# An elementwise layer-scale kernel: pieces of 40, 37, 40 and 11 rows, two large stores, and stores released by a load's landing

## Chip, cores, metric

One core of one Trainium2 chip. The metric is the device time of one execution in microseconds. "Span" is the time from the first to the last instruction in a profile; the time lies about 1.3 us above it. All runs told here are of the fast state, at a granted clock of 1.0. Ratios are the mean time of one kernel's fast runs over the mean of the other's of the same rounds, so they are not quite the ratios of the medians that stand beside them.

A packet is one record of a DMA engine's work in the trace: start, length, size, queue. The records as kept do not name the engine, so what is said of one engine is either a sum over all packets divided by 16 ("the mean engine", "an engine") or found by matching each packet's start to an earlier packet's end. A load or store is issued by its queue, runs as packets, and lands when its completion signal comes. A hole is time in which the DMA engines stand still.

## The reference

```python
B, S, D = 1024, 16, 512          # all bfloat16
def reference(x, y, gamma):      # x, y: [B, S, D]; gamma: [D]
    return x + gamma * y
```

33.55 MB must be read and 16.78 MB written, and there is one product and one sum per element.

## The kernel before

Each of 128 partitions holds 128 rows of 512 elements (1 KB a row). y stays whole in SBUF and becomes the result in place; x passes through a buffer of 64 rows. gamma is spread over the partitions by one matmul with a column of ones. The load queue (SP) and the store queue (ACT) are lists; VectorE makes a product and a sum per piece.

```python
PIECES = [32, 32, 32, 32]
X_AT = [0, 32, 0, 32]            # where a piece of x lies in its buffer
X_AFTER = [-1, -1, 0, 1]         # the sum that must be done before it may be overwritten
SP = [('x', 0), ('y', 0), ('x', 1), ('y', 1), ('y', 2), ('x', 2), ('y', 3), ('x', 3)]
# ('s', first piece, last piece, sum that releases it)
ACT = [('g',), ('s', 0, 0, 2), ('s', 1, 1, 2), ('s', 2, 2, 2), ('s', 3, 3, 3)]
# ... cut ...
            need = X_AFTER[args[0]] if kind == "x" else args[2] if kind == "s" else -1
            if need > known:
                eng.wait_ge(s_add, need + 1)
# ... cut ...
    for c in range(n):
        yt = y_sb[:, piece(c), :]
        _take(s_y[c], 16, nc.vector)
        nc.vector.tensor_tensor(
            out=yt, in0=yt, in1=gamma_sb[:, None, :].to_broadcast([P, PIECES[c], D]), op=MULT
        ).then_inc(s_dve, 1)
        _take(s_x[c], 16, nc.vector)
        _take(s_dve, 1, nc.vector)
        nc.vector.tensor_tensor(out=yt, in0=x_tile(c), in1=yt, op=ADD).then_inc(s_add, 1)
```

The first three stores are held back until the third sum (index 2) is done, although the first piece is ready much earlier, so that loads go first and stores after.

## Time and profile before

| | before |
|---|---|
| time, median of 3 runs | 120.31 us (120.3 to 120.99) |
| profiled execution: time, span | 120.87 us, 119.5 us |

The lines of the profile and their reading stand in the prediction below.

### The profile page before, as it was taken

The numbers are of one execution on the slowest core, as the hardware profiler recorded it, in microseconds if no ns is written. First come the engines' busy times: TensorE is split into PE (matmuls) and PEld (weight loads), VectorE is DVE, ScalarE is ACT, GpSimd is POOL, SyncE is SP. The second block draws the span as 40 slices with busy tenths as digits, with TensorE's granted clock in tenths as the row PEclk, the third lists the DMA queues.
The fourth block names the chain that finished last, engine by engine and source line by source line (L and its number), as shares of the span: only waits on it lengthen the run. The fifth ranks groups of instructions, "written<-read, shape, count | busy, mean of one in ns | idle before, by whom it ended". The sixth has DMA issues, their size and how long they took to land. (4 is left out here: it accounts for less than half of the span.)

```text
span 119.5 us, 84 instructions
## 1 busy us (share of the span) xinstructions
PE 0.6 (0%) x1; PEld 0.1 (0%) x1; DVE 70.2 (59%) x10; POOL 0.2 (0%) x4
## 2 busy tenths in 40 slices
PE   0100000000000000000000000000000000000000
PEld 0000000000000000000000000000000000000000
DVE  0100000699999289999999999999999600000000
POOL 0000000000000000000000000000000000000000
DMA  7989898998998989898989999898989898989995
GB/s 208 494 373 504 351 526 351 384 493 351 384 493 351 526 351 526 351 515 362 493 384 471 406 428 450 384 493 351 526 351 526 351 526 351 515 362 471 406 471 230
DMA packets 1730, 50.33 MB, mean 421 GB/s; under 512 B 193, under 2 KB 194, under 8 KB 194
## 3 DMA queue, kind: packets, MB, share of 16 engines
q1 hardware_dynamic: 1152, 33.55, 66.4%
q10 hardware_dynamic: 578, 16.78, 32.5%
HBM read 33.56 MB, written 16.78 MB: 421 GB/s over the span
## 5 line engine op out<-in xcount | busy, mean ns | idle before, releaser
L115 DVE TENSOR_TENSOR y_sb<-y_sb,gamma_sb 128x16384 bf16<-128x16384 bf16 x4 | 34.8, 8688 | 18.4 <-DVEq L22 18.4
L120 DVE TENSOR_TENSOR y_sb<-x_sb,y_sb 128x16384 bf16<-128x16384 bf16 x4 | 34.8, 8692 | 0.6
L109 DVE CAST gamma_sb<-gamma_ps 128x512 bf16<-128x512 f32 x1 | 0.7, 692 | 3.4 <-DVEq L22 3.4
L104 DVE MEMSET ones_row<- 1x128 bf16 x1 | 0.2, 165 | 2.0 <-PEq L38 2.0
L107 PE MATMUL gamma_ps<-gamma_row,ones_row 1*128 1x512 bf16 x1 | 0.6, 580 | 4.8 <-PEq L22 4.8
L107 PEld LDWEIGHTS gamma_ps<-gamma_row,ones_row 1*128 1x128 bf16 x1 | 0.1, 100 | 4.8 <-issue 4.8
L149 POOL MEMSET const-bfloat16-1.0<- 128x1 bf16 x1 | 0.1, 101 | 0.0
L149 POOL MEMSET const-uint8-127<- 128x1 uint8 x1 | 0.1, 101 | 0.0
L149 POOL MEMSET const-float32-0.0<- 128x1 f32 x1 | 0.1, 98 | 0.2 <-issue 0.2
L149 POOL MEMSET const-float32-1.0<- 128x1 f32 x1 | 0.1, 98 | 0.0
## 6 DMA issues: line engine op xcount, KB each, us to landing
x_sb<-in_x_dram SPq DMA_DIRECT2D x4, 4096.0 KB, 21.5
y_sb<-in_y_dram SPq DMA_DIRECT2D x4, 4096.0 KB, 35.4
out_dram<-y_sb ACTq DMA_DIRECT2D x4, 4096.0 KB, 23.8
gamma_row<-in_gamma_dram ACTq DMA_DIRECT2D x1, 1.0 KB
```

Of the source, the lines that this page charges most:

```text
L104: nc.vector.memset(ones_row, 1.0).then_inc(s_ones, 1)
L107: nc.tensor.matmul(gamma_ps, ones_row, gamma_row, start=True, stop=True).then_inc(s_ps, 1)
L109: nc.vector.tensor_copy(out=gamma_sb, in_=gamma_ps).then_inc(s_dve, 1)
L115: nc.vector.tensor_tensor(out=yt, in0=yt, in1=gamma_sb[:, None, :].to_broadcast([P, PIECES[c], D]), op=MULT).then_inc(s_dve, 1)
L120: nc.vector.tensor_tensor(out=yt, in0=x_tile(c), in1=yt, op=ADD).then_inc(s_add, 1)
L149: nc = _bacc.Bacc("TRN2", target_bir_lowering=False, num_devices=1)
```

## The change

The intent: let the stores start when the loads are nearly through, by a signal from the loads themselves and not by a sum that happens to end then, so that pieces may have any size; and use fewer, larger transfers (7 loads and 2 stores in place of 8 and 4). The buffer of x grows from 64 to 77 rows. "64 KB" is per partition.

```diff
-PIECES = [32, 32, 32, 32]
-SP = [('x', 0), ('y', 0), ('x', 1), ('y', 1), ('y', 2), ('x', 2), ('y', 3), ('x', 3)]
-ACT = [('g',), ('s', 0, 0, 2), ('s', 1, 1, 2), ('s', 2, 2, 2), ('s', 3, 3, 3)]
+PIECES = [40, 37, 40, 11]
+# ('x', first row, end row, place in the buffer), ('y' or 's', first row, end row)
+SP = [('x', 0, 40, 0), ('y', 0, 40), ('x', 40, 77, 40), ('y', 40, 77), ('y', 77, 128), ('x', 77, 117, 0), ('x', 117, 128, 40)]
+ACT = [('g',), ('s', 0, 64), ('s', 64, 128)]
+RELEASE = ('x', 77, 117, 0)
 # ... cut: bookkeeping of which rows a load or a store meets ...
+            if kind == "s" and not went:
+                _take(s_go, 1, eng)          # ACT, ahead of the first store
+                went = True
 # ... cut ...
+    _take(s_load[RELEASE], 16, nc.tensor)    # TensorE sees the landing ...
+    nc.tensor.sem_inc(s_go, 1)               # ... and tells ACT
+    nc.tensor.sem_inc(s_rel, 1)              # ... and VectorE
```

## The prediction

> **What bounds the kernel now.** I read the page first, parts 1 to 3, then the table of windows, then the order of time around the hand-over from loads to stores, and last the packet records of the trace (start, duration and size of each DMA packet).
>
> ```profile
> PE 0.6 (0%) x1; PEld 0.1 (0%) x1; DVE 70.2 (59%) x10; POOL 0.2 (0%) x4
> DMA  7989898998998989898989999898989898989995
> q1 hardware_dynamic: 1152, 33.55, 66.4%
> q10 hardware_dynamic: 578, 16.78, 32.5%
> L115 DVE TENSOR_TENSOR y_sb<-y_sb,gamma_sb 128x16384 bf16<-128x16384 bf16 x4 | 34.8, 8688 | 18.4 <-DVEq L22 18.4
> L120 DVE TENSOR_TENSOR y_sb<-x_sb,y_sb 128x16384 bf16<-128x16384 bf16 x4 | 34.8, 8692 | 0.6
> ```
>
> The two DMA queues took 66.4 + 32.5 = 98.9% of the span of all 16 engines: loads first (q1), stores second (q10). VectorE is busy 59%, and it sets nothing as long as it is in time. So the bound is the DMA engines, and the question is only which of their microseconds are not transfer at full rate. The windows answer that (columns: stretch, length, busy time of the engines, clock, DMA share, GB/s; 12.10 us is ten packets of 32 KB per engine):
>
> ```profile
> 0.00:1.00 1.00, 0.00 (x0) 0.00 (x0) 0.00 (x0) 0.20 (x4) 1.00 0.12 33
> 1.00:3.07 2.07, 0.00 (x0) 0.00 (x0) 0.17 (x1) 0.00 (x0) 1.00 1.14 348
> 3.07:15.20 12.13, 0.58 (x1) 0.10 (x1) 0.69 (x1) 0.00 (x0) 1.00 1.01 435
> 19.00:31.10 12.10, 0.00 (x0) 0.00 (x0) 8.89 (x2) 0.00 (x0) 1.00 0.97 395
> 43.20:55.30 12.10, 0.00 (x0) 0.00 (x0) 11.95 (x2) 0.00 (x0) 1.00 1.00 433
> 67.40:79.50 12.10, 0.00 (x0) 0.00 (x0) 11.95 (x3) 0.00 (x0) 1.00 1.00 433
> 79.50:91.60 12.10, 0.00 (x0) 0.00 (x0) 11.95 (x2) 0.00 (x0) 1.00 1.00 433
> 103.70:115.80 12.10, 0.00 (x0) 0.00 (x0) 0.00 (x0) 0.00 (x0) 1.00 1.00 433
> ```
>
> Loads alone, loads beside VectorE, and stores all run at 433 GB/s, and the window across the hand-over (79.50 to 91.60) does too: there is no hole between loads and stores. By the packet records, a 32 KB packet follows the last one on its engine every 1.210 us. The 96 packets of an engine at that pace are 116.2 us. The rest of 119.5 is four items: about 1.1 us before the first packets; 0.7 us by which each engine's first packet is long (1.93 against 1.21 us); about 1.1 us in a slow stage from 16 to 42 us, where packets take 1.22 to 1.33 us (the window with 395; its cause isn't shown, and VectorE's work isn't it, for later windows have more of that at 433); and about 0.5 us from the last packet's end to the end of the span. They add up to 119.6.
>
> The hand-over, in order of time (three merged issues, the third alone, then the last):
>
> ```profile
> 77.05 8.68 DVE L115 TENSOR_TENSOR y_sb<-y_sb,gamma_sb 128x16384 bf16<-128x16384 bf16 x1
> 77.17 4.06 ACTq L95 DMA_DIRECT2D out_dram<-y_sb  x3
> ...
> 78.04 3.19 ACTq L95 DMA_DIRECT2D out_dram<-y_sb  x1
> ...
> 85.88 8.69 DVE L120 TENSOR_TENSOR y_sb<-x_sb,y_sb 128x16384 bf16<-128x16384 bf16 x1
> 94.61 0.34 ACTq L95 DMA_DIRECT2D out_dram<-y_sb  x1
> ```
>
> The third addition ends at 77.13 and releases three stores at 77.17. The packet records have the first store packets at 80.1, just as the load queue runs dry (its last packet ends at 80.4). The last store is issued at 94.61, while the three before it keep the engines busy to about 109: 14 us of slack.
>
> **What the Trainium skill says.** "DMA: Bandwidth & Descriptors", section "Where 436 GB/s comes from", gives a ceiling of 435.2 GB/s for the 16 ports; the 433 here is 99.5% of it. The same page, "Why small descriptors are slow", names a fixed cost of about 3 cycles per packet. The difference between 1.210 us and 32768 B at 27.2 GB/s (1.2047 us) is 5.6 ns per packet, which is of that order. Its section "Queues, rings and completion order" says an engine switches between queues after each packet. This trace doesn't show such mixing: no store packet ran in the 2.9 us after the issue while load packets were left. "Advanced Engine Details and Errata", "VectorE Performance Modes", allows tensor_tensor two elements a cycle at best; 16384 elements in 8.69 us is 1.89 per ns, so the additions and products can't be made faster by other piece sizes.
>
> **The change, part by part.** The bytes are the same: 33.55 MB in, 16.78 MB out.
>
> 1. Fewer, larger packets. The loads go from 8 to 7 and the stores from 4 to 2, of 8 packets per engine each: 96 become 72. 24 x 5.6 ns = 0.13 us saved. It assumes that 64 KB per partition is one packet; if it is cut, less.
> 2. The work before the first packet, the long first packet and the tail are untouched: same two early loads, same kind of last store. 0.
> 3. The release of the stores. Now: landing of the load of rows 77 to 117 of x, passed on by TensorE. One row costs an engine 8 KB, 0.3012 us. I start the first packets at 1.14, add 0.71 for the long first one, 0.045 per load for its packets, the slow stage of 1.1 us, and 0.53 from last packet to landing (before: y's first load has its last packets end at about 21.4, landing 21.93). Landings: x(40) 14.5, y(40) 27.0, x(37) 38.7, y(37) 50.0, y(51) 65.4, x(40) 77.5, x(11) 80.9. So the stores are released at about 77.7 against 77.17, and the load queue runs dry at 80.3. An issue needs about 1 us to the first packet (first load of the program: 0.0 to 0.99), so both arrive while loads still run. No hole before, none after: 0.
> 4. VectorE. 8.69 / 32 = 0.2716 us per row and pass; a sum follows its product by 0.15, a product follows the sum before with no gap. First product 27.1, first sum ends at 49.0. Second product waits for y(37): 50.1; second sum ends at 70.4. The third pair needs no more waiting (x(40) at 77.5, its sum begins at 81.4) and ends at 92.2, the fourth (11 rows, 2.99 each) at 98.2. That is 3.7 us later than the 94.57 of before.
> 5. Waits of loads for room in x_sb: x(40) goes out after the first sum, 49.0, long before the queue reaches it at 65; x(11) after the second, 70.4, reached at 77. No hole: 0.
> 6. The second store (rows 64 to 128) needs the last sum, 98.2, so its packets can begin at about 99.2. The engines end the first store at 80.3 + 64 x 0.3012 = 99.6. Slack about 0.4 us, where before had 14. If the slow stage is shorter, VectorE moves with it, because y(37)'s landing starts the second pair, down to about 49.0: the slack doesn't shrink much. I take 0 for the hole, 0.1 for the chance of one.
>
> Sum: -0.13 + 0.1, so about zero: span 119.5, and the time, with the same surroundings, 120.31 - 0.03, rounded to 120.2 because the removed packets are surer than the hole.
>
> **The rivals.** First, a hole between the two stores: the issue to first packet takes longer than 1 us in a busy queue, or VectorE ends later. For it: slack is only 0.4 us, and the first packet of a fresh queue is 0.7 us long. Against it: landings and durations on VectorE repeat to 0.01 us. It would cost 0.3 to 1.5 us: up to 121.8. Second, the slow stage goes or grows, since the engines now walk 40 and 37 KB runs instead of 32 KB: without it 119.2, doubled 121.4. Against: it is not tied to an address, for it begins within y's first load and ends within y's second. Third, the stores mix with the load of 11 rows packet for packet: at release it has about 2.6 us left, 1.6 when the stores can begin, perhaps 4 of its 11 KB packets per engine. Each may wait for a 64 KB packet, 2.41 us, so that it lands at about 90. The fourth sum needs it at 95.2, so this costs nothing. Fourth, large packets are cheaper than I think: the ceiling of 435.2 GB/s bounds that, 0.4 us in all beside the 116.2.
>
> **Range and chances.** Everything that could be gained is the 0.4 us of packets and the 1.1 of the slow stage: 1.5 us, 1.2%, so 118.8 is the floor that I can derive and faster by 2% (117.9) is out of reach unless the first packets change too. Slower by 2% (122.7) needs a hole or slow stages of 2.4 us, which no number supports. Before's own three runs span 0.7 us. Range 119.4 to 121.0. Faster 0.01, same 0.97, slower 0.02.
>
> **What would show it.** Right: two queues together still at 98.5 to 99% of the span; windows of 433 throughout; first store issue near 77.7, last sum ending near 98.2, second store's issue just after, no idle engine near 99.6. Fewer packets: 1730 - 16 x 27 (24 data, 3 semaphore) = about 1298. Wrong: an idle stretch near 80 or 99 in the DMA row; x(11) landing after 95 and VectorE waiting for it; the window of 19 to 31 us at 433 or below 380; packets of 64 KB at another rate than 27.1 GB/s per engine.

## The result and the profile after

The changed kernel takes 120.03 us (median of 6, 119.94 to 120.14) and the kernel before 120.46 us in the same rounds (6 runs, 120.24 to 120.99). The ratio is 0.996, 95% interval 0.9937 to 0.9982: the same at 2%, yet clear of 1. The page of the profile after, span 118.8 us: the row of DMA busy tenths, the packets, the two queues (packets, MB, share), and VectorE's two groups.

```profile
DMA  7999999999999999989696999998899889988890
DMA packets 1298, 50.33 MB, mean 424 GB/s; under 512 B 145, under 2 KB 146, under 8 KB 146
q1 hardware_dynamic: 1008, 33.55, 66.0%
q10 hardware_dynamic: 290, 16.78, 32.6%
L153 DVE TENSOR_TENSOR y_sb<-y_sb,gamma_sb 128x20480 bf16<-128x20480 bf16 (+2 forms) x4 | 34.8, 8688 | 20.6 <-DVEq L25 20.6
L162 DVE TENSOR_TENSOR y_sb<-x_sb,y_sb 128x20480 bf16<-128x20480 bf16 (+2 forms) x4 | 34.8, 8691 | 0.6
```

The two shares are 98.6%: full, as before. Packets fell from 1730 to 1298. VectorE's work is what it was, and it waits only for loads of y (20.6 us before products), not before sums (0.6). The windows of the profile after, cut at the boundaries of loads (8 packets of 40 KB, then 8 of 37 KB per engine; the columns are as in the prediction):

```profile
13.98:26.07 12.09, 0.00 (x0) 0.00 (x0) 0.00 (x0) 0.00 (x0) 1.00 1.00 432
26.07:37.25 11.18, 0.00 (x0) 0.00 (x0) 10.41 (x1) 0.00 (x0) 1.00 1.00 434
```

Where the kernel before had 395 GB/s in one stretch of its profile, this one has 432 and 434. By the packet records, packets above the usual length of their size, the first packet of each engine left out, cost 0.92 us an engine up to 60 us in the profile before (0.88 of it between 16 and 42 us) and 0.12 us here. The order of time at the hand-over and at the second store:

```profile
69.41 10.82 DVE L153 TENSOR_TENSOR y_sb<-y_sb,gamma_sb 128x20480 bf16<-128x20480 bf16 x1
77.07 0.37 ACTq L116 DMA_DIRECT2D out_dram<-y_sb  x1
80.38 10.82 DVE L162 TENSOR_TENSOR y_sb<-x_sb,y_sb 128x20480 bf16<-128x20480 bf16 x1
...
91.12 3.08 DVE L153 TENSOR_TENSOR y_sb<-y_sb,gamma_sb 128x5632 bf16<-128x5632 bf16 x1
94.35 3.09 DVE L162 TENSOR_TENSOR y_sb<-x_sb,y_sb 128x5632 bf16<-128x5632 bf16 x1
97.47 0.34 ACTq L116 DMA_DIRECT2D out_dram<-y_sb  x1
```

The release load landed at 76.72 and the first store was issued 0.35 us later, at 77.07. The first store packets ran at 79.16, while the last load packets ended at 79.61 and the last load landed at 80.10: no hole and no mixing. The second store was issued at 97.47, and the packet records have its first packets at 98.5 to 99.1 (mean 98.8), on average 2.44 us after the last ones of the first store began, the length of one such packet: no hole there either.

So the question is which part of the change gives the 0.4 us, and which parts only avoid a loss.

### The profile page after: what moved, and what is told of

Same layout as the page of the kernel before. It is cut to its first block, busy times and chain, and to the rows that moved or that the text cites. A ratio compares the mean times of both kernels' runs of the same rounds, so it can differ in the third digit from the quotient of the medians.

```text
span 118.8 us, 84 instructions
## 1 busy us (share of the span) xinstructions
PE 0.6 (0%) x1; PEld 0.1 (0%) x1; DVE 70.2 (59%) x10; POOL 0.2 (0%) x4
## 2 busy tenths in 40 slices
DMA packets 1298, 50.33 MB, mean 424 GB/s; under 512 B 145, under 2 KB 146, under 8 KB 146
## 5 line engine op out<-in xcount | busy, mean ns | idle before, releaser
L153 DVE TENSOR_TENSOR y_sb<-y_sb,gamma_sb 128x20480 bf16<-128x20480 bf16 (+2 forms) x4 | 34.8, 8688 | 20.6 <-DVEq L25 20.6
L162 DVE TENSOR_TENSOR y_sb<-x_sb,y_sb 128x20480 bf16<-128x20480 bf16 (+2 forms) x4 | 34.8, 8691 | 0.6
## 6 DMA issues: line engine op xcount, KB each, us to landing
x_sb<-in_x_dram SPq DMA_DIRECT2D x1, 1408.0 KB, 10.6
```

Of the source, the lines that this page charges most:

```text
L153: nc.vector.tensor_tensor(out=yt, in0=yt, in1=g, op=MULT).then_inc(s_dve, 1)
L162: nc.vector.tensor_tensor(out=yt, in0=xt, in1=yt, op=ADD).then_inc(s_add, 1)
```

## The experiments

Twelve runs were made in three calls of four, on one chip, each of six executions (five timed rounds and the profiled one); all were correct. Two of the twelve are the kernel before and one is the changed kernel, without an edit. The executions of the kernel before that ratios are taken against are the call's own, except that the second call (later release, earlier release, less slack, changed kernel again) has the first call's eleven and one more. "Over the changed kernel" always means over the 119.97 us of its second look, also for kernels of another call.

**The noise: the kernel before again.** No edit, run twice.

> The kernel before once more, unchanged. If the slow stage of loads (16 to 42 us, 1.1 us in all) belongs to its 32 KB packets, this profile shows it again and the span is near 119.5; if it is chance of one execution, it is absent or elsewhere, and the span is near 118.5 to 118.9. The ratio to before should be 1.000; what it differs by is the noise of the method.

> The kernel before a third time, in the same call as the three others, for its spread under the same conditions: 120.0 to 121.0, median 120.3 to 120.4. If it is tight this time, the spread goes with the hour or the chip and the comparison of spreads says nothing.

Measured: 120.39 us (119.99 to 120.84), ratio 0.9999, interval 0.9965 to 1.0032; and 120.37 us (120.06 to 121.16), ratio 1.0015, interval 0.9987 to 1.0043. The same window of the profile before, of the second and of the third look:

```profile
19.05:31.15 12.10, 0.00 (x0) 0.00 (x0) 8.94 (x2) 0.00 (x0) 1.00 0.96 390
```

```profile
19.05:31.15 12.10, 0.00 (x0) 0.00 (x0) 9.10 (x2) 0.00 (x0) 1.00 1.00 433
```

```profile
19.05:31.15 12.10, 0.00 (x0) 0.00 (x0) 9.08 (x2) 0.00 (x0) 1.00 1.00 433
```

The slow stage is not in every execution of the kernel: two later executions of the same code do without it, and their spans are 119.0 us against 119.5. But the kernel before has slow executions at all. Over 41 runs of it (in several calls) the times reach from 119.99 to 121.16, median 120.33, and 27 of 41 are over 120.24, which is the slowest of the changed kernel's twelve (119.94 to 120.24, median 119.99).

The two later profiles are themselves of executions above 120.24 (120.33 and 120.28), and the packet records show part of what they lose: the last one or two load packets of most engines, which run while the stores are being issued, are longer than usual. Over load packets that start after 72 us this makes 0.23 and 0.17 us an engine. In the first profile, which had the slow stage, it is 0.00; in the two profiles of the changed kernel 0.01 and 0.03.

**The changed kernel again.** No edit.

> The changed kernel once more on the same chip as these. Ratio 0.996 as in its first result; the profile without the slow stage if that goes with the packet sizes.

Measured: 119.97 us (119.95 to 120.24), ratio 0.9961, interval 0.9935 to 0.9987, as expected. The best run of the kernel before (119.99) and of the changed one (119.94) differ by 0.05 us. The gain of 0.4 us between medians is thus mostly slow time that the changed kernel's executions did not have, and hardly the time of a good one.

**The stores alone.**

```diff
 # in the kernel before
-('s', 0, 0, 2), ('s', 1, 1, 2), ('s', 2, 2, 2), ('s', 3, 3, 3)
+('s', 0, 1, 2), ('s', 2, 3, 3)
```

> The kernel before with its four stores made two (64 KB per partition), nothing else; still released by the third addition. If large store packets give the gain: 16 packets per engine fewer, 0.03 to 0.1 us, ratio 0.999 to 1.000. If the whole measured gain of 0.4 us came from the stores, ratio 0.996 to 0.997. If it came from the loads, ratio 1.000 and the slow stage stays.

Measured: 120.26 us (119.99 to 120.53), ratio 0.998, interval 0.9952 to 1.0008. The interval holds 0.996 as well as 0.999 and 1.000, so this run alone decides nothing about the stores. In its profile (120.4 us) the last load packets are long by 0.15 us an engine, as in the kernel before.

**The loads without the large stores.**

```diff
 # in the changed kernel
-('s', 0, 64), ('s', 64, 128)
+('s', 0, 32), ('s', 32, 64), ('s', 64, 96), ('s', 96, 128)
```

> The changed kernel with its two stores cut back into four of 32 KB; loads, pieces and release as changed. If the gain came from the loads: ratio 0.996 to 0.997, as the change, and no slow stage. If it came from the two large stores: ratio 0.999 to 1.000. The fixed cost per packet predicts 0.03 to 0.1 us over the changed kernel.

Measured: 120.02 us (119.97 to 120.24), ratio 0.9964, interval 0.9938 to 0.999. With four stores of 32 KB the gain is all there: 0.05 us over the changed kernel's 119.97. The large stores are not needed for it. The loads or the release carry it; no run put the old release beside the new loads, so these two were not parted.

**Twice as many packets.** Every load and store of the changed kernel is cut in two.

```diff
-SP = [('x', 0, 40, 0), ('y', 0, 40), ... ('x', 117, 128, 40)]
+SP = [('x', 0, 20, 0), ('x', 20, 40, 20), ('y', 0, 20), ('y', 20, 40), ('x', 40, 58, 40), ('x', 58, 77, 58), ('y', 40, 58), ('y', 58, 77), ('y', 77, 102), ('y', 102, 128), ('x', 77, 97, 0), ('x', 97, 117, 20), ('x', 117, 122, 40), ('x', 122, 128, 45)]
 # four stores of 32 rows; released by ('x', 97, 117, 20); the loads issued ahead of all else (EARLY) are four in place of two, the same rows
```

> The changed kernel with every load and every store cut in two, so 144 packets per engine in place of 72, same pieces and same rows for the release. By the fit of packet pitch against size in the changed kernel (11 KB at 0.417 us, 64 KB at 2.416 us), 2 to 6 ns per packet: 0.15 to 0.4 us longer than the changed kernel, ratio to before 0.998 to 1.000. If packets cost nothing by themselves: 0.996. If small load packets bring the slow stage, over 1.002, and the profile shows packets that are long for their size.

Measured: 120.51 us (120.45 to 120.57), ratio 1.0002, interval 0.9976 to 1.0028; the page:

```profile
DMA packets 2595, 50.33 MB, mean 422 GB/s; under 512 B 290, under 2 KB 291, under 8 KB 547
```

That is 0.54 us over the changed kernel (120.51 - 119.97) for 72 more packets an engine, 7.5 ns each, more than the fit of packet lengths had promised. The runs are tight (0.12 us apart), and no slow stage shows: small load packets as such do not bring it. If 7.5 ns held for the 24 packets between the kernel before and the changed one, that would be 0.18 us; the 0.05 us between the best runs (2 ns a packet) and the 0.05 us for the 16 packets of the four stores (3 ns) say less, but these are differences of the size of the noise. The packet records lie between: the packets of an engine at their usual lengths make 116.2 us in the kernel before and 116.1 in the changed one, 0.11 us or 5 ns a packet. I take 0.05 to 0.18 us.

**A later release.**

```diff
-RELEASE = ('x', 77, 117, 0)
+RELEASE = ('x', 117, 128, 40)
```

> The changed kernel released by the landing of the very last load (11 rows of x) in place of the last but one. If the choice of the load matters as step 3 says: landing near 80.1, 0.35 us for the relay, about 1 us from issue to first packet: stores begin near 81.4 in place of 79.7, so a hole of 1.7 us and about 121.7 us, ratio 1.010. If store descriptors are slow to start for another reason (queues that drain first), less than 0.5 us.

Measured: 121.86 us (121.82 to 122.01), ratio 1.0115, interval 1.0086 to 1.0144: 1.89 us over the changed kernel. The order of time:

```profile
80.32 10.83 DVE L162 TENSOR_TENSOR y_sb<-x_sb,y_sb 128x20480 bf16<-128x20480 bf16 x1
80.50 0.37 ACTq L116 DMA_DIRECT2D out_dram<-y_sb  x1
```

The store is issued at 80.50, 3.4 us after 77.07. Its first packets come at 81.37 (all 16 engines by 81.52); the last load packets had ended at 79.81. The hole is made of the landing (80.15, after the last packets' end), the relay (0.35) and 0.87 us from issue to first packet; the mean engine stands still for 1.99 us between 79.0 and 81.6, and that goes into the time in full.

**An earlier release.**

```diff
-RELEASE = ('x', 77, 117, 0)
+RELEASE = ('y', 77, 128)
```

The load lands at 64.5, but the first store also needs the second sum, which ends at 69.4 and so sets the time.

> The changed kernel released by the landing of y's last load, so that the second addition, near 69.5, sets the time of the first store; loads have then 10 us to go. If stores and loads mix packet for packet, store packets begin near 70.5 and the landings of x's last two loads come up to 10 us later (near 88 and 90), VectorE waits, its last addition ends over 100, and the second store leaves a hole or not; 120 to 124 us. If stores only run after the loads already queued, as the trace before suggested, the loads land as they did (76.7 and 80.1) and the time is that of the changed kernel, ratio 0.996.

Measured: 125.7 us (125.6 to 125.87), ratio 1.0432, interval 1.0402 to 1.0461; worse than either expectation. The times from issue to landing of x's last load, first in the changed kernel, then in this one:

```profile
x_sb<-in_x_dram SPq DMA_DIRECT2D x1, 1408.0 KB, 10.6
```

```profile
x_sb<-in_x_dram SPq DMA_DIRECT2D x1, 1408.0 KB, 31.0
```

And this kernel's row of DMA busy tenths, who waited, and VectorE's two sums that waited, from three views of it:

```profile
DMA  7999999998999899979979999899999407797777
```

```profile
DVE y_sb L162 <- DVEq L25: 6.7, 2, 4.7
```

```profile
84.77 10.82 DVE L162 TENSOR_TENSOR y_sb<-x_sb,y_sb 128x20480 bf16<-128x20480 bf16 x1 [4.66 <-DVEq L25]
...
100.64 3.09 DVE L162 TENSOR_TENSOR y_sb<-x_sb,y_sb 128x5632 bf16<-128x5632 bf16 x1 [2.04 <-DVEq L25]
```

The store is issued at 69.41 and its first packets run at 73.5, in the midst of loads: from there an engine's packets of both queues take turns, mostly one by one, in places two (at most three) of a queue in a row. Load packets thus wait for store packets of 64 KB: the load of rows 77 to 117 of x landed at 84.53 and not at 76.72, and the third sum waited for it (4.66 us); x's last load, of 11 KB packets, landed at 100.40 and not at 80.10. The last sum waited for that one and ended at 103.7; the first store had landed at 99.6; and the digits "40" in the row are the hole before the second store's packets at 104.6: the mean engine stands still for 5.0 us of the 5.7 that are lost. The rest goes with packets that are longer while the queues take turns (1.0 us an engine between 60 and 82 us). So here the release too early cost more than the one too late. The kernel before had escaped that: its stores too were issued 3.2 us before the loads ended, but their packets took 2.9 us to come up behind the loads already queued.

**Less slack for the second store.**

```diff
-ACT = [('g',), ('s', 0, 64), ('s', 64, 128)]
+ACT = [('g',), ('s', 0, 56), ('s', 56, 120), ('s', 120, 128)]
```

> The changed kernel with stores of 56, 64 and 8 rows: the first store runs dry 2.4 us earlier (near 96.4) while the second still waits for the last addition (issue near 97.5). If issue to first packet is 1 us, a hole of 2.1 us: 122.1 us, ratio 1.014. If the wait to first packet is shorter in a running program, 1.1 to 1.6 us. If the second store is not what the engines wait for, 120.0.

Measured: 121.96 us (121.89 to 122.02), ratio 1.0123, interval 1.0097 to 1.0149: 1.99 us over the changed kernel. VectorE's last sum and the two stores after it (merged):

```profile
94.18 3.09 DVE L162 TENSOR_TENSOR y_sb<-x_sb,y_sb 128x5632 bf16<-128x5632 bf16 x1
97.30 0.82 ACTq L116 DMA_DIRECT2D out_dram<-y_sb  x2
```

The second store's first packets begin at 98.15 to 98.29, 0.85 us after its issue. By the packet records the mean engine stands still for 1.96 us between 96.0 and 98.6, which is the whole loss; the same count over 97.5 to 99.5 in the changed kernel gives 0.03 us. The changed kernel is thus within some tenths of a microsecond of such a hole: there, the second store's packets could begin at about 97.47 + 0.85 = 98.3, and the engines took them up at 98.47 (the first) to 98.8 (the mean).

**Which loads bring the slow executions?** First the changed kernel with loads of 32 rows at the start:

```diff
-PIECES = [40, 37, 40, 11]
+PIECES = [32, 32, 53, 11]
-SP = [('x', 0, 40, 0), ('y', 0, 40), ... ('x', 117, 128, 40)]
+SP = [('x', 0, 32, 0), ('y', 0, 32), ('x', 32, 64, 32), ('y', 32, 64), ('y', 64, 128), ('x', 64, 96, 0), ('x', 96, 117, 32), ('x', 117, 128, 53)]
 # released by ('x', 96, 117, 32)
```

> The changed kernel (its code, release, two 64 KB stores, last piece of 11 rows) with the first four loads at 32 rows as before, then y's 64 rows and x in 32, 21 and 11. If loads of exactly 32 KB bring the slow packets that make the runs of before differ by 1 us (119.99 to 121.05): runs spread over 0.5 us or more, median 120.2 to 120.4, and excess packet time in some profile. If the spread comes from something else that the change removed (store packets, release): six runs within 0.3 us, median 120.0 to 120.1 (80 packets per engine in place of 72 are worth 0.06 us).

Measured: 120.17 us (120.0 to 120.44), ratio 0.9995, interval 0.9976 to 1.0014. The spread of 0.44 us is between the two expectations. The ratio looks as if the gain were gone, but the kernel before was fast in this call (median 120.17 of its eleven, 120.41 in the first call), the interval overlaps that of the changed kernel (0.9935 to 0.9987), and the changed kernel was not run in this call. By its own time this kernel lies between the medians of the two (119.99 and 120.33), with two of six executions above 120.24. That the loads' sizes matter is suggested by this, not shown. Its profile, of a run of 120.01 us, shows no slow stage. Then the kernel before with other sizes:

```diff
-PIECES = [32, 32, 32, 32]
+PIECES = [33, 31, 33, 31]     # b_odd;  X_AT = [0, 33, 0, 33]
+PIECES = [36, 28, 36, 28]     # b_36;   X_AT = [0, 36, 0, 36]
```

> The kernel before with pieces of 33, 31, 33, 31 rows in place of four of 32; everything else, also 96 packets per engine and the release by the third addition, as before. If exact 32 KB packets bring the slow packets: six runs within 0.3 us, median 120.1 to 120.2 (the changed kernel and 24 packets of 7.5 ns). If it is the number of packets or the code of before: spread 0.5 us or more and median 120.2 to 120.4 as before.

> The kernel before with pieces of 36, 28, 36, 28 rows. As for the odd pieces, a second instance of sizes that are not 32 KB, and multiples of 4 KB unlike those: tight and 120.1 to 120.2 if only the exact size of 32 KB matters. The third addition ends near 79, so the first store packets may come up to 0.3 us after the loads; that would be seen as idle time of the queues near 80, and is counted out.

Measured: 33 and 31 rows 120.56 us (120.11 to 121.38), ratio 1.0036, interval 1.0002 to 1.0069; 36 and 28 rows 120.68 us (120.58 to 120.79), ratio 1.0034, interval 1.0018 to 1.005. The odd sizes are as scattered as 32: the theory that exact 32 KB packets are the cause falls. The sizes 36 and 28 are tight, although packets (96), code and the rule of release are those of before; what they lose is a hole, as their store is issued late:

```profile
79.09 2.17 ACTq L95 DMA_DIRECT2D out_dram<-y_sb  x3
```

By the packet records the first store packets come at 79.96 to 80.11, the last load packets end by 79.81 and on most engines some tenths before: the mean engine stands still for 0.57 us between 79.0 and 80.3, which is about what its fastest run lacks (120.58 against 120.06 of the kernel before in the same call).

This hole leaves a rival standing. With 36 and 28 rows the first store packets meet no load packets, for the loads are over before they come. And the last load packets, long by 0.11 to 0.23 us an engine in four profiles (the kernel before in its second and third look, with two stores, and with 33 and 31 rows; not in its first look), have their usual length here (0.02 us) and in the changed kernel, with four stores and with loads of 32 rows (0.03 us at most), where the last load has packets of 11 KB. So the slow time may belong to the hand-over from large load packets to stores, and not to the sizes of the first loads; no run parts the two.

## Why the prediction was right, and where it wasn't

The time (120.03) lies in the range, and "the same" holds. That the number is so near is partly luck: the sum was -0.03 us on 120.31, the median of three runs of before (so 120.28, put down as 120.2), while in the rounds of the result before had 120.46. The forecast change is -0.03 to -0.1 us, the measured one -0.43. By its steps:

1. *Fewer packets, -0.13 us.* The count of 1298 came out exactly. The size of the term: 0.05 to 0.18 us, as above. (The 5.6 ns a packet are an estimate from the page's ceiling; 1.210 less 1.2047 us is 5.3 ns, and so the packets' bound of "0.4 us in all" should be 0.5.)
2. *Both ends untouched.* First packets 1.20 us after the start on average against 1.14; the first packet's excess 0.68 against 0.71 us; right.
3. *The release.* Predicted landing 77.5 and issue 77.7; measured 76.72 and 77.07, early because the slow stage of 1.1 us (0.88 by the packet records) that the sum carried along was absent. No hole, as predicted. The last-load experiment shows that this step was a real condition: 1.9 us depend on it.
4. *VectorE.* Sums predicted to end at 49.0, 70.4, 92.2 and 98.2; measured 48.64, 69.49, 91.20 and 97.44, again by the missing slow stage.
5. *Room in x's buffer.* No hole in the loads; right.
6. *The second store's slack, 0.4 us.* Measured 0.2 to 0.5 us, with the 0.85 us from issue to packet that the slack experiment gave in place of my 1 us. That experiment confirms the first rival as real, only not reached. Its reason that the first packet of a fresh queue is long does not hold for the stores: in both kernels their first packets have the usual length (1.21 and 2.42 us); only the first packets of the program are long. And landings do not repeat to 0.01 us: the release load landed at 76.55 to 76.78 us in four profiles with the same loads (changed kernel twice, later release, less slack).

Two steps failed. The first is in the second rival: "without it 119.2" took the slow stage of 1.1 us off 120.31, the median. But the profile is of an execution of 120.87 us; the median run did not hold that much of it. Off 120.87 it would have been 119.8, and the measured 120.03 is near that. In the sum itself the failed step is to carry the slow time of before over unchanged: three profiles of the kernel before (one with the stage, two without) show that it is not in every execution, and the changed kernel's profile has 432 and 434 GB/s where the first had 395. The prediction had named this, the window of 19 to 31 us at 433, as a sign of being wrong, and it came.

The second is in the third rival, which let mixed packets land the last load "at about 90" at no cost, after the remark that this trace doesn't show mixing. Mixing was there in the early release as soon as the store packets came up while loads were queued: it put the landing at 100.4 and cost 5.7 us. That release came 7.7 us before the one the rival spoke of (69.41 against 77.07), so the rival's own numbers were not put to the test. In the changed kernel itself it didn't arise, for the loads had 2.5 us left at the issue, and the store packets came 2.1 us after it.

What stays open is the cause of the gain: why kernels with loads of 31 to 33 rows have executions up to 1 us slower. Such executions came with 32, with 33 and 31, and more weakly with the first loads at 32 in the changed code; they did not come in six runs each with 36 and 28, with 20-row halves, or with 40 and 37 rows (five kernels). Of the profiles of such kernels only the very first fell on an execution 0.5 us or more above the best (120.87), and it lost its time at 16 to 42 us. Those of 120.28 to 120.4 us lost 0.11 to 0.23 us of theirs at the hand-over. The slowest ones (to 121.38) were not profiled, and six runs a kernel are few.

## What to carry to other kernels

When the DMA queues are at 99% of the span, ask first how much single executions of the same kernel differ, and take a second profile before a stage in one is called a property of the code; here the two kernels' best runs were 0.05 us apart and most of the gain was missing slow time, whose cause stays open. A store stream behind a load stream had a window for its release in this kernel: too late left a hole of landing, relay (the signal's way over TensorE) and issue (1.9 us), too early let large store packets take turns with the last small loads and starved what waited for them (5.7 us). The landing of the last load but one, with 2.5 us of loads still to run, hit that window: the store packets came 2.1 us after the issue. It no longer hangs on the end of the third sum, but the loads themselves still wait for sums to make room in x's buffer.

## What the Trainium skill lacked or had wrong

- "DMA: Bandwidth & Descriptors", section "Queues, rings and completion order", says that an engine turns from queue to queue after each packet. The early release agrees in the main (x's last load landed after 31.0 us in place of 10.6), but its packet records have two packets of a queue in a row in places, and once, on one engine, three. What the page lacks is the delay before it begins: store packets ran 4.1, 2.9 and 2.1 us after the issue behind queued loads (early release, before, after), against 0.85 to 0.87 us with idle queues (less slack, late release).
- The same page, "Why small descriptors are slow", names a fixed cost per packet and works it out for a descriptor of 256 bytes only. Here packets of many KB bore one too: 72 more packets of 5 to 32 KB per engine cost 0.54 us, 7.5 ns each, while other comparisons gave 2 to 5 ns.
- No page that I found tells of executions of one kernel, alone on its core at full clock, whose loads run at 390 GB/s for 12 us in one execution and at 433 in others, nor of load packets that are long while stores are issued behind them (0.11 to 0.23 us an engine in four profiles). Whether this goes with load sizes (119.99 to 121.16 us in 41 runs with 32 rows, 119.94 to 120.24 in 12 with 40 and 37) is not shown.
